# A new order for all operations and loads of a gated linear-attention kernel with a maxout layer

## The chip, the cores and the metric

The kernel runs on one core of a Trainium2 chip. The core has five engines, each with its own queue, which they work through in order and in parallel to one another: TensorE (PE: matmuls and transposes, results in PSUM), VectorE (DVE), ScalarE (ACT), GpSimd (POOL, which works on SBUF only here) and SyncE (SP), which here issues every DMA. They wait for one another through semaphores. The metric is device time in microseconds, as the median of several runs.

## What is computed

A recurrent attention with a state of 48x48 per batch and head, and a feed-forward layer on its output. The sizes are batch 4, 8 heads, 768 steps, head width 48; 3072 tokens of width 384 go into a layer of width 1024.

```python
for t in range(S):
    kt, vt, rt, wt = (k[:, :, t], v[:, :, t], r[:, :, t], w[:, :, t])
    cur = np.einsum('bhd,bhe->bhde', u[None] * kt, vt)
    y[:, :, t] = np.einsum('bhd,bhde->bhe', rt, state + cur)
    state = wt[:, :, :, None] * state + np.einsum('bhd,bhe->bhde', kt, vt)
x = y.transpose(0, 2, 1, 3).reshape(B * S, H * D)
out = np.maximum(x @ w1, x @ w2) @ w_out
```

The kernel does the recurrence in pieces of 256 steps: logarithms of `w` are summed with a triangular matrix, `r` and `k` are scaled by the exponentials of these sums, and what is left are matmuls inside the piece and one product with the state of the pieces before it. For the layer it uses max(a, b) = max(a - b, 0) + b: the weights w1 - w2 (`wd_sb`) go through a relu, and w2 @ w_out is folded into one matrix (`wc_sb`).

## The kernel before

The work is cut into eight units (`UNITS`): units 0 to 3 are the first 256 steps of one batch each, units 4 and 5 the second 256 steps of two batches each, units 6 and 7 the third. Unit 0 is cut into two halves of four heads. What each engine does, and in which order, stands in one list, `ORDER`, written out in the file; the loop at the end of `_body` takes one entry after the other and emits its instructions. An engine's queue is thus the entries of that engine in the order of the list; SP's queue is the order of the loads and stores. An entry is a name, numbers, and for some a letter behind `@` that names the engine: a for ACT, d for DVE, p for POOL.

The entries, with unit u, batch b of the unit, half y:

- `load.u.w` (and k, r, v; `load.0.w.0` and `load.0.w.1` are the halves): L372. `wload.x.n` loads rows n of w1 or w2 (L285), `woload` w_out (L290), `os` stores (L743). All are on SP. `row` and `wl` take a row of sums through DRAM onto partitions.
- `zero`, `mask`, `tri`, `ident`, `identb`, `identq`: constants and cleared areas. `zero.s.1` clears a half of `S_b` (L263), `zero.M` the off-diagonal part of a score buffer.
- `wp` multiplies two steps' w, `ln` takes the logarithm (L387), `hi` and `lo` split it into two parts for units 3 to 7, `ex` is the triangular sum on PE (L398, or L395 and L396 in two parts), `mz` adds (L440), `e0` and `ie` are exponentials, `wt` and `we` give the decay of the whole piece.
- `rw`, `kw` multiply r and k by w; `rk`, `ru`, `dg` make the term with u (products on DVE or POOL, a sum on DVE), which `dd` and `di` place on a diagonal of the score buffer M; `vb` casts v.
- `scale.u.x.b.y` scales r (x = 0) or k (x = 1); for r one input is in PSUM, for k both are in SBUF. `tr` transposes r and k on PE for units 0 to 4 and `te` copies that from PSUM (`RK`); units 5 to 7 use a transposing DMA instead (`dt`, L582).
- `sc` makes scores (L641), `mk` copies them with a mask into M (L650), `kv` updates the state (L596), followed by `st`, `sm`, `sb`; `ya` (L688) and `yi` (L675) make the output, `xe` copies it from PSUM as bf16.
- `wdiff` makes w1 - w2, `w2turn` and `w2take` transpose w2 (L307), `wocast` casts w_out, `wfold` makes the folded matrix (L318) and `wctake` copies it. `gt` is the first product of the layer (L706), `rl` its relu (L717 on ACT, L719 on DVE), `op` the second product (L725 and L729), `oe` its copy from PSUM.
- `hot.8.n` is a group of eight matmuls whose result nobody reads (L234). There are six of them.

PSUM is shared out in two kinds of tiles, four banks "G" for `hot`, `ex`, `tr`, `w2turn`, `wfold`, `gt`, `op`, and two double banks "Y" for `sc`, `kv` and the output. A new tile takes the bank whose last reader stands earliest in `ORDER` and waits for that reader.

A product on POOL of 768 elements or more is split in two (`by_two`), on DVE it is not:

```python
        if e == "d" or n < 2 * HD:
            op(o, a, b)
        else:
            m = o.shape[1] // 2
            for g in (slice(0, m), slice(m, 2 * m)):
                op(o[:, g], a[:, g], b[:, g])
```

Of the kernel before, what the change touches and what calls it, by code (L numbers as in the profile page):

```python
# [797 lines left out]
```

## Time and profile before

| | |
|---|---|
| median of 3 runs | 152.08 us (151.09 to 153.25) |
| the profiled execution | 149.86 us |
| its span, first to last instruction | 148.2 us |
| mean granted clock of TensorE | 0.977 |
| ACT busy | 93.7 us (63%) |
| POOL busy | 76.4 us (52%) |
| read from HBM, written | 23.61 MB, 4.73 MB |
| DMA queue of the loads and stores | 81.6% of 16 engines' span |

The profiled execution is one run of its own, and it was shorter than the three timed ones; all views below are of it. In the views, a busy PE need not be PE at its peak, since matmuls are pipelined. The page gives the busy share of each engine in forty slices of the span, each digit in tenths. The chain that ended last is followed back from the last instruction, at each step to what released it. "issue" in it is time in which the engine waited for nothing that the profile shows.

### The profile page before, as it was taken

The page shows a single profiled execution, that of the slowest core. Times are in us where ns is not written, and L with a number is a line of the kernel's source. Part 1 is how long each engine was busy: PE and PEld are TensorE (multiplying, and loading weights), DVE is VectorE, ACT ScalarE, POOL GpSimd, SP SyncE. Part 2 cuts the span into 40 slices and gives each one's busy share as a digit, 9 for nine tenths or more (in the row PEclk, how much of TensorE's full clock was granted, in tenths as well). Part 3 has the DMA queues.
Part 4 walks back from the last instruction along what each step waited for, and adds up shares of the span by engine and source line. Part 5 has one row for each costly group of instructions (what it writes and reads, how often), then busy time and mean ns, then how long its engine had stood idle before and what let it go on. Part 6 is the DMA issues. An engine that isn't in the chain of part 4 may idle for free.

```text
span 148.2 us, 5523 instructions
## 1 busy us (share of the span) xinstructions
PE 137.9 (93%) x2404; PEld 85.0 (57%) x2404; DVE 115.0 (78%) x160; ACT 93.7 (63%) x173; POOL 76.4 (52%) x94
## 2 busy tenths in 40 slices
PE   4969969989989999999999999999999999999991
PEld 1344654765766676777665456654567445664550
DVE  2259849979999989999999999999599879623100
ACT  3252295679963999998779945578557772245321
POOL 8769729591393047337993069970899600000000
PEclk9996895999999999999999999999999999999999
DMA  4999999989989953999839879999894688360042
GB/s 110 297 357 302 338 269 374 372 247 269 250 234 287 237 123 87 316 286 215 223 68 245 179 170 272 286 233 282 186 250 131 90 172 241 110 214 5 0 164 106
DMA packets 71188, 31.85 MB, mean 215 GB/s; under 512 B 66294, under 2 KB 70391, under 8 KB 71163
## 3 DMA queue, kind: packets, MB, share of 16 engines
q1 hardware_dynamic: 71162, 31.49, 81.6%
q8 instruction: 19, 0.31, 0.9%
q14 instruction: 7, 0.05, 0.1%
HBM read 23.61 MB, written 4.73 MB: 191 GB/s over the span
## 4 chain that ended last, share of the span: by engine, by line
PE 62%; DVE 13%; ACT 7%; DMA 5%; POOL 4%; issue 4%; SPq 2%; POOLq 1%; DVEq 0%; ACTq 0%
PE G L706 15%; PE G L729 15%; PE G L234 7%; PE G L725 6%; DVE M L650 5%; PE Y L688 4%; PE Y L641 3%; DMA lw<-in_w_dram 3%; PE G L318 3%; ACT RK L168 3%; DMA RK<-rp 2%; PE Y L675 2%; PE G L398 2%; POOL kp L180 2%; PE Y L596 1%
## 5 line engine op out<-in xcount | busy, mean ns | idle before, releaser
L729 PE MATMUL G<-wo_sb,gT 128*128 128x384 bf16 x192 | 35.1, 326 | 0.0
L706 PE MATMUL G<-xT,wd_sb 128*128 128x256 bf16 (+1 forms) x192 | 33.9, 326 | 0.1
L650 DVE CAST_PREDICATED M<-mask,Y 128x1024 bf16<-128x1024 int32 (+1 forms) x26 | 28.7, 1133 | 3.0 <-PE Y L641 2.9
L717 ACT ACTIVATE gT<-G 128x512 bf16<-128x512 f32 x41 | 23.4, 599 | 6.2 <-PE G L706 5.9
L729 PEld LDWEIGHTS <-gT 128*128 128x128 bf16 x192 | 18.8, 98 | 12.4
L706 PEld LDWEIGHTS <-wd_sb 128*128 128x128 bf16 x192 | 18.1, 98 | 12.5 <-issue 0.5
L180 POOL TENSOR_TENSOR rku<-rku,u_b 128x384 f32<-128x384 f32 x12 | 12.5, 1065 | 13.1 <-DVE rku L176 13.1
L234 PE MATMUL G<-S_b 128*128 128x512 bf16 x48 | 15.4, 488 | 2.1 <-DVE S_b L263 2.1
L725 PE MATMUL G<-wc_sb,xT 128*128 128x384 bf16 x72 | 15.7, 328 | 0.0
L168 ACT COPY RK<-G 128x1024 bf16<-128x1024 bf16 x12 | 11.8, 1016 | 6.0 <-PE G L565 6.0
L168 ACT COPY osb<-G 128x384 f32<-128x384 f32 x13 | 6.2, 477 | 12.7 <-PE G L729 10.8
L180 POOL TENSOR_TENSOR kp<-lk,iE 128x384 bf16<-128x384 f32 x10 | 11.2, 1147 | 1.8 <-issue 1.8
L234 PEld LDWEIGHTS <-S_b 128*128 128x128 bf16 x48 | 5.6, 123 | 11.0 <-issue 6.6
L168 ACT CAST xT<-Y 128x768 bf16<-128x768 f32 x10 | 10.2, 1033 | 2.4 <-PE Y L688 1.4
L502 DVE TENSOR_REDUCE dg<-rku 128x16 f32<-128x768 f32 x12 | 11.0, 944 | 0.0
L180 POOL TENSOR_TENSOR lk<-lk,lw 128x384 f32<-128x384 f32 x6 | 6.3, 1070 | 7.4 <-DVE rku L176 7.4
L641 PE MATMUL Y<-RK 48*64 48x128 bf16 x384 | 8.9, 220 | 1.2 <-ACT RK L168 0.5
L516 DVE TENSOR_TENSOR M<-identq,gd 128x512 int32<-128x512 int32 x12 | 9.0, 753 | 1.2 <-ACT gd L168 1.0
L440 DVE TENSOR_TENSOR MZ<-G,lg 128x384 f32<-128x384 f32 (+1 forms) x13 | 6.5, 513 | 3.6 <-PE G L398 2.1
L641 PEld LDWEIGHTS <-RK 48*64 48x64 bf16 x384 | 6.3, 106 | 4.9 <-issue 3.2
L688 PE MATMUL Y<-M,vp 64*32 64x128 bf16 x768 | 8.7, 219 | 0.3 <-DVE M L650 0.3
L176 DVE TENSOR_TENSOR rp<-lr,G 128x768 bf16<-128x768 f32 (+2 forms) x11 | 8.7, 795 | 0.4 <-ACT W L486 0.3
(108 smaller groups left out, 234.7 us busy)
## 6 DMA issues: line engine op xcount, KB each, us to landing
lk<-in_k_dram SPq DMA_DIRECT2D x12, 384.0 KB, 4.2
lv<-in_v_dram SPq DMA_DIRECT2D x12, 384.0 KB, 5.9
lr<-in_r_dram SPq DMA_DIRECT2D x10, 384.0 KB, 5.7
lw<-in_w_dram SPq DMA_DIRECT2D x9, 384.0 KB, 5.9
out_dram<-osb SPq DMA_DIRECT2D x14, 192.0 KB, 2.3
gT<-in_moe_w_dram SPq DMA_DIRECT2D x4, 512.0 KB, 8.7
out_dram<-wb SPq DMA_DIRECT2D x10, 192.0 KB, 3.8
wso<-in_moe_w_out_dram SPq DMA_DIRECT2D x4, 384.0 KB, 6.2
```

What stands on the lines that cost most here:

```text
L168: (nc.scalar.copy if e == "a" else nc.vector.tensor_copy if e == "d" else nc.gpsimd.tensor_copy)(o, i)
L180: op(o[:, g], a[:, g], b[:, g])
L234: nc.tensor.matmul(t, zz[:, 0:P], zz[:, 0:512], start=True, stop=True)
L502: nc.vector.reduce_sum(s.dg[:, b].rearrange("p i h -> p h i"), s.rku[:, b], axis=AX.X)
L516: (nc.vector if en == "d" else nc.gpsimd).tensor_tensor(out=o, in0=m, in1=g.unsqueeze(3).to_broadcast([P, 2, H, Q // 2]), op=ALU.bitwise_and)
L641: nc.tensor.matmul(t[q * Q:(q + 1) * Q, e, p * P:(p + 1) * P].rearrange("s (i g) -> s i g", i=2), s.kT[d, b, j, y * n + p, q, :], s.rT[d, ...
L650: nc.vector.copy_predicated(t[:, :, 2 * n * y:2 * n * (y + 1)].rearrange("s i (p e) g -> s p e i g", e=2), mask[:, j].bitcast(I32).unsquee ...
L688: nc.tensor.matmul(lhsT=s.vp[g, b, 2 * p + e, j, m * 32:(m + 1) * 32], rhs=s.M[b, j][g, :, 2 * p + e, :], **into(s, b, q, p * 96 + (e + m) ...
L706: nc.tensor.matmul(t[:, m * n * P:(m + 1) * n * P].rearrange("c (b t) -> c b t", t=P), wd_sb[:, ko, fo * P:(fo + 1) * P], s.xT[:, 0:n, ko, :],
L717: nc.scalar.activation(o, i, AF.Relu)
L725: nc.tensor.matmul(t[:, 0:HD], s.xT[:, a, ko, :], wc_sb[:, ko, :], start=(ko == 0), stop=False)
L729: nc.tensor.matmul(t[:, 0:HD], s.gT[:, c:c + P], wo_sb[:, f, :], start=False, stop=(f == FO - 1))
```

## The change

Only the list `ORDER` is replaced. It has the same 652 entries before and after, in another order. 70 of them go to another engine: 21 from ACT to DVE, 16 from DVE to ACT, 15 from DVE to POOL, 12 from POOL to DVE, 3 from POOL to ACT and 3 from ACT to POOL. The order of the loads on SP changes with it: `load.0.w.1` comes first instead of fifth. Because the bank of a PSUM tile follows from the list, the bank that an operation waits for can be another one. In the part that is not shown, `scale.4.1.1.0`, `scale.5.1.0.0`, `scale.5.1.1.0`, `scale.6.1.0.0`, `rk.7.0` and `rw.7.0` go from DVE to POOL, and `rk.5.0`, `ru.6.0`, `ru.6.1`, `ru.7.1`, `kw.7.0` and `scale.7.1.1.0` from POOL to DVE; the other moves there are copies, casts and relus, mostly between ACT and DVE. The first part of the two lists, to where unit 4 begins, and their ends:

```diff
@@ -51,66 +51,66 @@
 ORDER = """
-zero.k.1@p zero.M.1@p load.1.w.0 zero.m@p mask zero.k.0@d load.0.w.0 u ident identb@p identq@a tri
-wp.0.0@p ln.0.0 zero.s.0@d hot.8.3 zero.o@p load.0.k wp.1.0@d load.0.w.1 load.0.r wp.0.1@d hot.8.0
-kw.0.1@p ln.0.1 ex.0.1 load.1.k ex.0.0 ln.1.0 wload.1.1 kw.0.0@p mz.0.0 ie.0.0 zero.v.1@d wt.0.0
-uspread mz.0.1 ie.0.1 e0.0.1 zero.v.0@d wt.0.1 rw.0.1@d rk.0.0@d scale.0.0.0.1@d utake@a hot.8.2
-we.0.0 load.1.r hot.8.1 rw.0.0@p ru.0.0@d zero.r@d e0.0.0 scale.0.0.0.0@d we.0.1 scale.0.1.0.1@p
-scale.0.1.0.0@p ex.1.0 load.2.w.0 tr.0.0.0 zero.s.1@p te.0.0.0@a tr.0.0.1 te.0.0.1@a w2turn.1.0
-load.0.v vb.0.0@a vb.0.1@p dg.0 load.1.v rk.1.0@d dd.0@a ru.1.0@d mz.1.0 sc.0.0.0.0 wload.1.2 kv.0
-dg.1 ie.1.0 w2take.1.0@a sc.0.0.1.0 kw.1.0@p w2turn.2.0 load.3.w.0 wp.2.0@d vb.1.0@a st.0.0@a ln.2.0
-di.0.0@d zero.M.0@p st.0.1 rw.1.0@d load.2.r wt.1.0 mk.0.0.0.0 sm.0@p w2take.2.0@a sc.0.0.1.1
-sc.0.0.0.1 mk.0.0.0.1 mk.0.0.1.1 ex.2.0 we.1.0 e0.1.0 hot.8.5 vb.1.1@a dd.1@a zero.v.2@d sb.0.0@a
-mz.2.0 scale.1.1.0.0@p scale.1.0.0.0@d ie.2.0 load.2.k rk.2.0@d w2turn.2.1 w2take.2.1@a tr.1.0.1
-kw.2.0@d e0.2.0 wload.1.0 rw.2.0@d kv.1 tr.1.0.0 woload.0 w2turn.1.1 te.1.0.1@a te.1.0.0@a
-w2turn.0.0 mk.0.0.1.0 scale.2.0.0.0@d st.1.0@a st.1.1 sb.1.0@a w2take.1.1@a sc.1.0.0.0 wp.3.0@p
-sc.1.0.1.0 scale.2.1.0.0@p tr.2.0.0 wload.0.2 sb.0.1@a tr.2.0.1 te.2.0.1@a wdiff.2@p load.2.v
-di.1.0@d mk.1.0.1.0 ln.3.0 wload.0.0 w2turn.0.1 w2take.0.1@a mk.1.0.0.0 trih@a vb.2.1@p ya.0.0.1.1
-vb.2.0@a yi.0.0 ya.0.0.0.0 sb.1.1@a ya.0.0.1.0 ya.0.0.0.1 w2take.0.0@d xe.0.0@a ya.1.0.1.0 hi.3@a
-ya.1.0.0.0 hot.8.4 yi.1.0 wdiff.0@d wload.0.1 wdiff.1@d gt.0.2 te.2.0.0@a lo.3@d gt.0.1 ex.3.0
-ru.2.0@d xe.1.0@a rl.0.2@a row.2 sm.1@d gt.1.1 load.3.r load.3.k rk.3.0@d gt.1.3 woload.2 mz.3.0
-wocast.0@a rl.0.1@a ie.3.0 sc.2.0.1.0 woload.1 dg.2 dd.2@a rl.1.3@d kv.2 rl.1.1@d gt.0.3 st.2.0@a
-rl.0.3@a woload.3 gt.1.0 st.2.1 gt.1.2 zero.M.2@p di.2.0@d e0.3.0 rw.3.0@p wocast.2@p load.3.v
-sc.2.0.0.0 scale.3.0.0.0@d kw.3.0@p mk.2.0.0.0 gt.0.0 mk.2.0.1.0 ru.3.0@d wocast.1@p wocast.3@a
-sb.2.0@a wfold.1 load.4.w.0 wp.4.0@d rl.1.0@a wfold.0 rl.1.2@a vb.3.1@d dg.3 wctake.0@a sb.2.1@a
-scale.3.1.0.0@p wfold.2 ln.4.0 hi.4@d wctake.2@a dd.3@d ya.2.0.1.0 wctake.1@a di.3.0@d lo.4@d
-rl.0.0@a row.3 ya.2.0.0.0 load.4.k load.4.r rk.4.0@d vb.3.0@p yi.2.0 kv.3 st.3.0@a st.3.1 xe.2.0@a
-tr.3.0.0 te.3.0.0@a op.1.1 rk.4.1@d oe.1.1@a tr.3.0.1 te.3.0.1@a gt.2.0 gt.2.2 rl.2.2@a rw.4.0@d
-gt.2.1 ru.4.1@p load.4.v wl.2 load.5.w.0 rl.2.1@a ex.4.0 mz.4.0 ex.4.1 wl.3 mz.4.1 row.4 rl.2.0@a
...
-xe.7.0@d gt.7.7 rl.7.7@a gt.7.0 gt.7.4 rl.7.4@a gt.7.5 gt.7.6 rl.7.5@a gt.7.2 rl.7.0@a rl.7.6@d
-os.6.3 os.6.0 gt.7.1 rl.7.1@a os.5.3 os.4.0 gt.7.3 rl.7.3@a rl.7.2@d op.7.1 oe.7.1@d os.7.1 op.7.2
-oe.7.2@a op.7.0 os.7.2 oe.7.0@a os.6.1 os.7.0 op.7.3 oe.7.3@a os.7.3
+zero.m@p load.0.w.1 load.1.w.0 u zero.o@p ident tri identb@p zero.r@d zero.k.1@p zero.s.0@d identq@a
+load.0.r hot.8.3 zero.s.1@p wp.0.1@p load.0.w.0 wp.1.0@d load.0.k load.1.k hot.8.0 zero.k.0@d ln.0.1
+ex.0.1 wp.0.0@d ln.0.0 uspread mz.0.1 e0.0.1 kw.0.0@d rw.0.0@p rk.0.0@d ex.0.0 ln.1.0 rw.0.1@p
+utake@a mz.0.0 kw.0.1@p ru.0.0@p zero.v.1@d wt.0.1 we.0.1 scale.0.0.0.1@d mask ex.1.0 ie.0.0 wt.0.0
+ie.0.1 mz.1.0 we.0.0 scale.0.1.0.1@d e0.0.0 hot.8.1 load.1.r tr.0.0.1 rk.1.0@d scale.0.0.0.0@d
+ru.1.0@p ie.1.0 scale.0.1.0.0@d dg.0 te.0.0.1@a kw.1.0@p dd.0@a wload.1.2 di.0.0@d zero.M.0@p wt.1.0
+we.1.0 hot.8.2 sc.0.0.0.1 load.0.v vb.0.0@a dg.1 e0.1.0 vb.0.1@a kv.0 load.1.v vb.1.1@a w2turn.2.0
+load.2.w.0 wp.2.0@d load.2.r st.0.0@a load.3.w.0 scale.1.1.0.0@p w2turn.2.1 dd.1@a rw.1.0@d
+scale.1.0.0.0@d sc.0.0.1.1 sb.0.1@a load.2.k st.0.1 ln.2.0 wload.1.0 tr.0.0.0 zero.v.0@d mk.0.0.0.1
+wload.1.1 wload.0.1 wp.3.0@p mk.0.0.1.1 wload.0.2 sb.0.0@d w2take.2.1@a vb.1.0@a ex.2.0 tr.1.0.0
+wload.0.0 kv.1 mz.2.0 te.0.0.0@a sc.0.0.1.0 load.2.v sc.0.0.0.0 rk.2.0@d zero.M.1@p rw.2.0@d
+w2take.2.0@a tr.1.0.1 sm.0@p kw.2.0@p st.1.0@a te.1.0.0@a st.1.1 ie.2.0 scale.2.1.0.0@p sb.1.0@a
+mk.0.0.1.0 e0.2.0 hot.8.5 w2turn.1.0 wdiff.2@p w2turn.0.1 mk.0.0.0.0 te.1.0.1@a row.2 w2take.1.0@a
+di.1.0@d w2take.0.1@a sc.1.0.0.0 scale.2.0.0.0@d sc.1.0.1.0 w2turn.0.0 mk.1.0.1.0 sb.1.1@a
+mk.1.0.0.0 w2turn.1.1 wdiff.1@d w2take.1.1@a tr.2.0.1 tr.2.0.0 zero.M.2@p wdiff.0@d te.2.0.0@a
+yi.1.0 ya.1.0.1.0 woload.0 yi.0.0 te.2.0.1@a vb.2.1@d ya.0.0.0.0 sm.1@d ya.0.0.1.1 ya.0.0.0.1
+ya.1.0.0.0 ya.0.0.1.0 load.3.r load.3.k woload.1 woload.2 hot.8.4 ru.2.0@d ln.3.0 hi.3@a lo.3@d
+rk.3.0@d xe.1.0@a kw.3.0@p gt.1.3 gt.1.0 w2take.0.0@a xe.0.0@a trih@a dg.2 gt.0.1 wocast.1@p
+rl.1.3@a rl.0.1@a vb.2.0@a rl.1.0@a ex.3.0 load.3.v mz.3.0 wocast.2@p gt.0.2 rl.0.2@d sc.2.0.1.0
+e0.3.0 woload.3 rw.3.0@d kv.2 wocast.0@a st.2.0@a ru.3.0@p gt.1.1 rl.1.1@a st.2.1 wocast.3@a gt.1.2
+ie.3.0 scale.3.1.0.0@p gt.0.3 load.4.w.0 wp.4.0@p dd.2@d sc.2.0.0.0 scale.3.0.0.0@d di.2.0@d
+mk.2.0.0.0 gt.0.0 wfold.2 vb.3.0@a rl.1.2@a dg.3 wfold.0 rl.0.3@a sb.2.1@a wctake.2@a rl.0.0@a
+wfold.1 row.3 dd.3@d tr.3.0.1 mk.2.0.1.0 wctake.1@d load.4.k load.4.r wl.2 tr.3.0.0 sb.2.0@a
+di.3.0@d ln.4.0 wctake.0@a hi.4@d ya.2.0.0.0 ya.2.0.1.0 load.4.v vb.3.1@p wl.3 load.5.w.0 yi.2.0
+rk.4.0@d kv.3 te.3.0.0@a xe.2.0@a st.3.0@a te.3.0.1@a lo.4@d op.1.1 ex.4.0 gt.2.0 oe.1.1@a rk.4.1@d
...
+oe.6.0@a yi.7.0 xe.7.0@a yi.7.1 xe.7.1@d op.6.1 oe.6.1@a os.6.1 oe.6.3@d gt.7.0 gt.7.3 rl.7.3@d
+os.6.0 rl.7.0@a os.6.3 gt.7.2 rl.7.2@a gt.7.7 rl.7.7@d gt.7.1 rl.7.1@d gt.7.6 rl.7.6@d gt.7.4 gt.7.5
+os.4.2 rl.7.5@d rl.7.4@a op.7.1 op.7.3 oe.7.3@d os.7.3 op.7.0 oe.7.0@a oe.7.1@a os.7.0 os.7.1 op.7.2
+oe.7.2@a os.7.2
 """.split()
```

62 lines of the change are left out of this document (31 added, 31 removed).

## The prediction

> **What bounds the kernel now.** I read the profile page first, then busy time by stretches of the span, then the chain that ended last, and last the timeline of the first 48 us. The page (lines of its first two parts):
>
> ```profile
> PE 137.9 (93%) x2404; PEld 85.0 (57%) x2404; DVE 115.0 (78%) x160; ACT 93.7 (63%) x173; POOL 76.4 (52%) x94
> PE   4969969989989999999999999999999999999991
> DVE  2259849979999989999999999999599879623100
> ```
>
> TensorE is busy for 93% of 148.2 us; its gaps lie in the first quarter. Busy time by stretches (PE, PEld, DVE, ACT, POOL, then granted clock, DMA share, GB/s) says how sharp that is:
>
> ```profile
> 12.00:16.00 4.00, 4.00 (x13) 1.41 (x12) 3.96 (x8) 0.17 (x1) 4.00 (x6) 0.57 1.13 309
> 24.00:28.00 4.00, 4.00 (x54) 2.17 (x52) 3.97 (x10) 1.24 (x3) 2.24 (x3) 0.75 1.07 373
> 36.86:144.93 108.07, 106.45 (x1978) 66.93 (x1978) 89.30 (x113) 72.78 (x127) 51.01 (x51) 1.00 0.79 192
> ```
>
> From 36.86, the first product with the folded first weight (L706), to 144.93, the last matmul, PE idles 1.62 us in 108.07. Before that the clock falls twice. The chain that ended last (start, us, what):
>
> ```profile
> 11.42 5.16 PE G L234 x16
> ...
> 36.86 0.78 PE G L706 x6
> ...
> 40.58 0.65 issue
> ...
> 118.08 3.68 DMA RK<-rp
> ...
> 144.96 0.48 ACT wb L168
> ```
>
> L234 is the filler ("hot"): 5.16 us of it sits on the chain while `ex.1.0` (L398) is queued behind. So the time is the start of the packed stretch (36.86), the stretch, and a tail of 3.2 us (144.96 to 148.2). The profiled execution took 149.86 us, 1.66 more than its span and 2.22 under the median of 152.08; I take the difference from the profile and put it on the median.
>
> **The change, part by part.** Both lists hold the same 652 operations, so no work goes. After the first L706 product the same products follow, but for `yi.1.0` (12 small matmuls), which moves ahead of it. Two things can change the time: when that product starts, and what stalls in the packed stretch. The tail ends in `op`, a copy on ACT and one store in both: nothing.
>
> *First loads.* The rows of the timeline (start, us, engine, line, what, idle before and its releaser):
>
> ```profile
> 2.06 5.30 PE L234 MATMUL G<-S_b 128*128 128x512 bf16 x16 [2.06 <-DVE S_b L263]
> 4.21 0.56 DVE L176 TENSOR_TENSOR lg<-lw 128x384 f32<-128x384 f32 x1 [2.20 <-DMA lw<-in_w_dram]
> 5.86 0.59 POOL L176 TENSOR_TENSOR lg<-lw 128x192 f32<-128x192 f32 x1
> 7.12 0.36 DVE L176 TENSOR_TENSOR lg<-lw 128x192 f32<-128x192 f32 x1 [2.36 <-DMA lw<-in_w_dram]
> 7.52 0.78 ACT L387 ACTIVATE lg<-lg 128x192 f32<-128x192 f32 x2 [0.67 <-DVE lg L176]
> 8.03 0.89 PE L398 MATMUL G<-lg,tri 128*128 128x192 f32 x4 [0.66 <-ACT lg L387]
> 14.00 1.38 POOL L263 MEMSET S_b<- 128x1536 bf16 x1
> ```
>
> `load.0.w.1` goes from fifth to first in SP's queue: it lands by about 4.2 (the first load now does) instead of 7.12. But its `wp.0.1` goes to POOL, behind set-up fills that now include the 1.38 us clearing of S_b, and `load.0.w.0` becomes fifth, with the same bytes ahead of it as `load.0.w.1` had: 7.1 again. POOL reached `wp.0.0` at 5.86; without zero.M.1 and the mask, with zero.s.1, it reaches `wp.0.1` near 4.7. With 0.59 and a logarithm of 0.39, and even a wait on DVE's own product, `ex.0.1` is ready by 6.4. The sixteen fillers hold PE to 7.2. So 8.03 becomes 7.2: 0.8 us of the 2.9 the load gives.
>
> *The middle of the front.* `ex.1.0` now stands ahead of the fillers hot.8.1 and hot.8.2, so it leaves at about 9.4 instead of 16.42. What is late next is POOL: it is given `ru.0.0` and `ru.1.0`, which DVE did, and loses the products `scale.0.1.0.*`. Rows:
>
> ```profile
> 10.29 0.94 DVE L176 TENSOR_TENSOR rku<-lr,lk 128x768 f32<-128x768 f32 x1
> 10.42 1.27 POOL L176 TENSOR_TENSOR kp<-lw,iE 128x192 bf16<-128x192 f32 x1 [1.17 <-ACT iE L460]
> 11.53 0.35 DVE L176 TENSOR_TENSOR rp<-lr,G 128x192 bf16<-128x192 f32 x1 [0.29 <-ACT W L486]
> 11.65 0.59 POOL L176 TENSOR_TENSOR kp<-lk,iE 128x192 bf16<-128x192 f32 x1
> 2.79 1.39 POOL L186 TENSOR_SCALAR_AFFINE_SELECT mask<-mask 64x64 f32<-64x64 f32 x6
> 20.95 0.95 POOL L257 MEMSET M<- 128x1024 bf16 x1 [3.39 <-DVE M L516]
> 23.83 1.00 POOL L176 TENSOR_TENSOR kp<-lk,iE 128x384 bf16<-128x384 f32 x1
> L180 POOL TENSOR_TENSOR rku<-rku,u_b 128x384 f32<-128x384 f32 x12 | 12.5, 1065 | 13.1 <-DVE rku L176 13.1
> ```
>
> POOL's list from about 10.3 (when `kw.0.1` is through) is ru.0.0 2.13, mask 1.7 (1.39 and its fill of 0.31), ru.1.0 2.13, kw.1.0 1.0, zero.M.0 0.95, scale.1.1.0.0 2.0: 9.9 us, to 20.2. That is the good end. The first two POOL rows give the bad one: a 128x192 product takes 0.59 beside a DVE product that reads PSUM (11.53), and 1.27 beside one with both inputs in SBUF (10.29): it loses about 0.7 of that one's 0.94. Four such DVE operations now fall on this list (scale.0.1.0.1, scale.0.1.0.0, both about 0.65, rk.1.0 0.94, di.0.0 0.7), so it ends up to 2.7 later, at 22.9. I take 22.9, because the rows for just this pairing show the loss. The Trainium skill's page "SBUF — State Buffer" says that a DVE instruction with two SBUF inputs shuts out a GpSimd instruction that reads SBUF for its whole length, and one with at most one does not. These rows agree (1.27 against 0.59); by the full block the list would end at about 23.1 and the sum be -2.2.
>
> `scale.1.1.0.0` gates `tr.1.0.0`, and behind that ACT works without a pause:
>
> ```profile
> L168 ACT COPY RK<-G 128x1024 bf16<-128x1024 bf16 x12 | 11.8, 1016 | 6.0 <-PE G L565 6.0
> L168 ACT CAST wb<-G 128x512 bf16<-128x512 f32 x5 | 2.9, 582 | 1.7 <-PE G L307 1.7
> L168 ACT CAST xT<-Y 128x768 bf16<-128x768 f32 x10 | 10.2, 1033 | 2.4 <-PE Y L688 1.4 <-PE Y L675 1.0
> 34.46 2.35 DVE L176 TENSOR_TENSOR wd_sb<-gT 128x1024 bf16<-128x1024 f32 x2
> 29.67 2.96 POOL L180 TENSOR_TENSOR wd_sb<-wst 128x512 bf16<-128x512 f32 x2
> ```
>
> Four `te` of 1.0, three `w2take` of 0.58, seven copies and exponentials of 0.34 to 0.53 (3.1 together), `xe.1.0` 1.03: 9.9 us, after 1.0 us for `tr.1.0.0` and `kv.1`, and I add 0.5 for the filler hot.8.5 in front of `w2turn.1.0`. So the first L706 product starts at 22.9 + 11.4 = 34.3 (at 20.2 it would be 31.6, but the same 0.5 grows to 1.9 if the filler falls in a half-clock stretch: 33.0). DVE has its `wdiff` by then: the three products ru.0.0, ru.1.0 and w2take.0.0 that it loses (2.8 us together) outweigh the halves it gains, and I get 33.9 for wdiff.0; wdiff.2 on POOL, blocked meanwhile, 34.3. Weights landed well before in the old run (the two `wdiff` on DVE waited for nothing), and fewer bytes stand ahead of the last one now. **Front: 36.8 to 34.3, minus 2.5; ends 0 and minus 3.8.**
>
> *The packed stretch.* The 0.65 inside `kv.2` (chain at 40.58) is "issue": no engine and no transfer released it, so I leave it where it is, at nothing. The 0.3 or so that PE waits after the transfer of `RK` (chain at 118.08) should go: its chain ran through POOL's two scalings of unit 7, and the second goes to DVE. A new wait stands at `ex.4.0`: three L706 products that came before it come after it, and its `wp.4.0` moves to POOL:
>
> ```profile
> 47.51 0.94 DVE L176 TENSOR_TENSOR lg<-lw 128x768 f32<-128x768 f32 x1
> 62.49 1.95 POOL L180 TENSOR_TENSOR lg<-wso 128x384 f32<-128x384 f32 x2
> 43.00 2.41 POOL L180 TENSOR_TENSOR kp<-lk,iE 128x384 bf16<-128x384 f32 x2
> 50.79 0.95 DVE L413 SCALAR_TENSOR_TENSOR wst<-lg,wst 128x768 f16<-128x768 f32 x1
> ```
>
> 0.94 becomes 1.95, behind a scaling of 2.41 that itself waits for `ie.3.0`. I get wp.4.0 at 46.3 and what follows it (a logarithm of some 0.8, hi 0.6, then rk.4.0 and lo of 0.95 on DVE, and a pause of 0.5) at 50.1. PE is there at 49.3: 34.3, then the 8.1 us that the old run took from its first L706 product to `wfold` less one small product, three `wfold`, two `tr`, unit 2's `ya` and `yi`, `kv.3`, `op.1.1`, 15 in all. Cost 0.8; nothing if POOL is on time. Everything on PE is queued behind it, so the stall is paid in full. DVE gives up wp.4.0, ru.3.0, scale.4.1.1.0 and both scale.5.1 (0.95 each, as at 47.51) and takes rk.5.0, rw.3.0 and some relus and copies (about 4): lighter by a little under 1 us, of which I count 0.4 as gained, since DVE stands on the chain only from 55 to 75. The other swaps of copies between ACT and DVE (0.5 to 0.7 either way) lie beside packed PE work: nothing, while each stays ahead of its bank's next use.
>
> **Sum:** -2.5 (front) - 0.3 (RK) + 0.8 (ex.4.0) - 0.4 (DVE) = -2.4 us; 149.86 becomes 147.5, and 152.08 becomes 149.7.
>
> **Rivals.** *POOL is on time* (its reads miss the four DVE operations): the front gives 3.8 and `ex.4.0` costs nothing: -3.8 - 0.3 - 0.4 = -4.5, 147.6. For it: blocking was seen on POOL products alone, and the mask is six short selects. *The front gives nearly nothing*: POOL slips 2 us more than I count, since the mask beside rk.1.0 is not shown in the old run: -0.4, 151.7. A third half-clock stretch in the front costs about as much: eight fillers take 3.4 us at 0.43 each (of the 16 in 5.30, half were slow) instead of 1.7: -0.7, 151.4. The Trainium skill's page "TensorE: Matmul & The Clock Gate", Part 1, has the clock halve after a window of some 3.4 us without work, counted freely of the kernel; the stretches at 0.57 and 0.75 agree in kind, and by it a third is possible as the front keeps its pauses. *Slower*: `wp.4.0`. It ended at 48.45 on DVE; if POOL ends it 5.5 us later than my 46.3, at 51.8, PE stands that much longer at `ex.4.0` and the sum passes +3: 155.2 and up, about 156. For it: POOL is the slower engine there by a factor of two and has five operations ahead of it. Against it: from 34.3 these are some 10 us with one late input, `ie.3.0`. *The change does nothing*, because the mask, the clock and POOL together give back the 2.4: 152.
>
> **How the numbers follow.** Main case 0.46 (148.2 to 151.0), POOL on time 0.20, the front gives nearly nothing (POOL, clock, or no effect) 0.26, slower 0.08. The likeliest gives 149.7. About 2% is what a measurement of this kernel can tell from no change: below 149.04 lie the case on time and some 0.4 of the main one, 0.38; above 155.1 lies 0.07; between them 0.55. The range, 146.8 to 153.0, runs from below the case on time to past no change, by about the 1 us by which runs of one kernel differ from their median (151.09 to 153.25); what it leaves out is the slower case and the tails.
>
> **What would show it.** Right: the first L398 near 7.2; `ex.1.0` ahead of the fillers; POOL's rku products at 128x384 taking over 1.0 each before 18; first L706 near 34; a wait of PE on L395 after the first `op`; no wait of PE on `RK` in unit 7. Wrong: first L706 after 36, or idle PE over 3 us behind it.

## The result, and the profile after

The changed kernel took 151.53 us (median of 20 runs, 149.92 to 156.79); the kernel before, on the same chip, 150.37 us (20 runs, 148.4 to 153.25). The ratio is 1.0151, 95% interval 1.0117 to 1.0185. It is taken over undisturbed executions alone, here and below, and so need not be the quotient of the medians. The forecast was 149.7, a gain of 2.4 us; the change costs 1.5% by the ratio, some 2 us, and 1.2 us by the two medians. The profiled execution of after took 151.67 us, its span 150.0 us (before: 149.86 and 148.2).

The first lines of the page of after, and its rows of PE and of the granted clock:

```profile
PE 137.7 (92%) x2401; PEld 84.6 (56%) x2404; DVE 119.4 (80%) x164; ACT 92.8 (62%) x168; POOL 84.1 (56%) x99
PE   4979998869999999999939999999999999999991
PEclk9995999999999999999996899999999999999999
```

In before the gaps of TensorE lay in the first quarter. Here there is a 3 in the middle (slice 21, from 75 us), and behind it the clock falls to 6 and 8 tenths. Read beside each other, the starts of the same operations in both timelines (an ordinary table, us; operations counted off against `ORDER`) say when the lead came and went:

```
operation            before    after    lead of after
ex.0.1 (L398)          8.03     6.96     1.07
ex.1.0 (L398)         16.42     9.25     7.17
first L706            36.79    35.27     1.52
op.3.0 (L725)         74.98    72.09     2.89
op.3.1 (L725)         78.34    79.02    -0.68
kv.5                  85.74    87.13    -1.39
last matmul, its end 144.93   146.77    -1.84
```

At 72 us after led by 2.89. Between `op.3.0` and `kv.5` it lost 4.28. The two orders are not quite level at these two places: when `op.3.0` starts, before has already done the 64 matmuls of `ya.4.1` (0.75 us) that after does later, and when `kv.5` starts, before has done `gt.4.5` and `ex.6.0` (1.07 us). Like for like the lead went from 2.1 to -2.5, and some 0.6 of this came back behind `kv.5`. The timeline of PE in after over that place (start, us, line, what, idle before and its releaser):

```profile
72.58 1.46 PE L729 MATMUL G<-wo_sb,gT 128*128 128x384 bf16 x8
73.98 0.53 PE L675 MATMUL Y<-RK,S_b 128*32 128x128 bf16 x24
74.44 0.42 PE L688 MATMUL Y<-M,vp 64*32 64x128 bf16 x32
75.08 0.43 PE L688 MATMUL Y<-M,vp 64*32 64x128 bf16 x32 [0.22 <-DVE M L650]
75.44 0.53 PE L675 MATMUL Y<-RK,S_b 128*32 128x128 bf16 x24
75.90 0.57 PE L688 MATMUL Y<-M,vp 64*32 64x128 bf16 x43
78.74 0.35 PE L688 MATMUL Y<-M,vp 64*32 64x128 bf16 x21 [2.28 <-issue]
79.02 0.66 PE L725 MATMUL G<-wc_sb,xT 128*128 128x384 bf16 x3
79.52 2.21 PE L729 MATMUL G<-wo_sb,gT 128*128 128x384 bf16 x8
```

And the same work in before:

```profile
73.72 0.75 PE L688 MATMUL Y<-M,vp 64*32 64x128 bf16 x64
...
74.98 0.66 PE L725 MATMUL G<-wc_sb,xT 128*128 128x384 bf16 x3
75.48 1.46 PE L729 MATMUL G<-wo_sb,gT 128*128 128x384 bf16 x8
76.87 0.86 PE L675 MATMUL Y<-RK,S_b 128*32 128x128 bf16 x48
77.67 0.75 PE L688 MATMUL Y<-M,vp 64*32 64x128 bf16 x64
78.34 0.66 PE L725 MATMUL G<-wc_sb,xT 128*128 128x384 bf16 x3
78.84 1.46 PE L729 MATMUL G<-wo_sb,gT 128*128 128x384 bf16 x8
```

The old list had 64 of the small matmuls of `ya.4` (L688), then `op.3.0`, then the rest. The new one has all 176 small ones of `ya.4` and `yi.4` in a row. In the middle of one operation, after 43 of 64 like matmuls with the same inputs, TensorE stands idle for 2.28 us (a "stand", from here on), and the releaser is "issue": no engine, no transfer. Then `op.3.1` takes 2.50 instead of 1.80 and the products behind it are slow too. The window of after from 80 to 84 us (PE, PEld, DVE, ACT, POOL, then granted clock, DMA share, GB/s) shows why:

```profile
80.00:84.00 4.00, 4.00 (x14) 1.66 (x12) 2.20 (x5) 2.03 (x4) 0.00 (x0) 0.57 0.86 144
```

and the same window of before:

```profile
80.00:84.00 4.00, 4.00 (x20) 1.84 (x19) 4.00 (x7) 3.61 (x9) 0.00 (x0) 1.00 1.26 186
```

14 matmuls instead of 20, at a clock of 0.57.

**Where the stands lie.** The page shows that TensorE's instructions themselves come by DMA (queue, kind: packets, MB, share):

```profile
q8 instruction: 19, 0.31, 0.9%
```

0.31 MB in 19 packets is 16 KB each; 2404 matmuls and as many weight loads are 4808 instructions, 253 a packet. I counted the instructions of TensorE ahead of every stand named issue of 0.3 us or more in the timelines of PE of this study: 35 of them, in 15 of the 17 traces. The count modulo 256 (what is left over after division by 256) lies between 178 and 186 in all 35 (the same place, but for a few missing records). So the stands lie at the bounds between blocks of 256 instructions. And each ends 1.23 to 1.59 us after a packet of this queue has ended. Nine of the 35 (us, from the trace's DMA records; "own work" is the time from the entry into the block of 256 to the stand):

```
kernel, place       entered   packet starts   ends    TensorE goes on   stand   own work
before, kv.2         34.03       38.49       39.79        41.23         0.65     6.55
after, ya.0          27.07       30.36       31.49        32.78         0.80     4.91
after, ya.4          74.45       76.47       77.44        78.74         2.28     2.01
a_again, ya.4        74.34       76.55       77.50        78.90         2.87     1.69
a_op31, ya.4         72.70       75.22       76.16        77.67         1.12     3.85
a_load7late, ya.4    74.56       75.06       76.51        77.98         1.74     1.69
b_dense, ya.4        73.49       75.05       76.47        77.91         2.53     1.89
a_halves, yi.6      110.11      111.09      112.09       113.46         1.71     1.64
b_shift72, yi.6     128.09      128.99      129.96       131.25         1.71     1.45
```

So the theory (A): the next block is asked for only when TensorE has entered the one before it; ahead of these 35 stands the packet started 0 to 4.5 us after that, took 0.9 to 1.45, and 1.2 to 1.6 later the block ran. A block with less work than this sum leaves TensorE standing, above all one of 128 small matmuls. The rivals: (B) a late operand that the profile doesn't name, (C) the clock gate (what lowers the granted clock) stopping TensorE by itself.

The first clause of A is too strong. In `after` three of the 19 packets started 0.3 to 3.1 us before TensorE entered the block (the last one at 141.90, the entry at 144.97). And four short blocks of 1.6 to 1.8 us of work did not stand, or for no more than 0.24 us: those at unit 5 in `a_again`, `a_kfirst`, `after` and `a_load7late`, where the packet had started 0.3 to 0.8 us before the entry. So the work in a block alone does not decide; when its packet starts does too, and what starts it is not shown.

### The profile page after: what moved, and what is told of

Its sections match the earlier page's. It is cut to its first block, busy times and chain, and to the rows that moved or that the text cites. A ratio compares the mean times of both kernels' runs of the same rounds, so it can differ in the third digit from the quotient of the medians.

```text
span 150.0 us, 5532 instructions
## 1 busy us (share of the span) xinstructions
PE 137.7 (92%) x2401; PEld 84.6 (56%) x2404; DVE 119.4 (80%) x164; ACT 92.8 (62%) x168; POOL 84.1 (56%) x99
## 4 chain that ended last, share of the span: by engine, by line
PE 59%; DVE 12%; DMA 10%; issue 7%; POOL 5%; SPq 3%; ACT 2%; DVEq 0%; POOLq 0%
PE G L706 19%; PE G L729 15%; PE G L725 6%; DVE M L650 6%; PE Y L688 4%; DMA lv<-in_v_dram 4%; DMA lk<-in_k_dram 4%; PE Y L641 3%; PE G L234 3%; SPq L372 3%; DMA WL<-row 2%; POOL lg L180 2%; PE Y L675 2%; PE Y L596 1%; DVE rku L176 1%
## 5 line engine op out<-in xcount | busy, mean ns | idle before, releaser
L706 PE MATMUL G<-xT,wd_sb 128*128 128x256 bf16 (+1 forms) x192 | 34.8, 332 | 0.0
L717 ACT ACTIVATE gT<-G 128x512 bf16<-128x512 f32 x39 | 22.5, 598 | 14.4 <-PE G L706 14.0
L706 PEld LDWEIGHTS <-wd_sb 128*128 128x128 bf16 x192 | 18.7, 99 | 13.5 <-issue 2.0
L180 POOL TENSOR_TENSOR kp<-lk,iE 128x384 bf16<-128x384 f32 x16 | 17.2, 1101 | 3.1 <-DVE lk L176 1.5
L234 PE MATMUL G<-S_b 128*128 128x512 bf16 x45 | 13.9, 454 | 2.2 <-DVE S_b L263 2.1
L688 PE MATMUL Y<-M,vp 64*32 64x128 bf16 x768 | 9.4, 219 | 3.6 <-issue 3.3
L516 DVE TENSOR_TENSOR M<-identq,gd 128x512 int32<-128x512 int32 x12 | 10.8, 918 | 0.5 <-ACT gd L168 0.5
L168 ACT COPY osb<-G 128x384 f32<-128x384 f32 x11 | 5.2, 476 | 9.5 <-PE G L729 9.4
L688 PEld LDWEIGHTS <-vp 64*32 64x32 bf16 x768 | 7.0, 90 | 6.2 <-issue 5.4
L176 POOL TENSOR_TENSOR S_f<-T,W 128x192 f32<-128x192 f32 (+1 forms) x5 | 3.4, 689 | 11.4 <-ACT W L488 8.1
L387 ACT ACTIVATE lg<-lg 128x768 f32<-128x768 f32 (+2 forms) x9 | 5.6, 625 | 6.5 <-DVE lg L176 2.7
L719 DVE TENSOR_SCALAR gT<-G 128x512 bf16<-128x512 f32 x9 | 6.1, 689 | 3.2 <-PE G L706 3.1
```

The lines of the kernel that those rows point to most:

```text
L168: (nc.scalar.copy if e == "a" else nc.vector.tensor_copy if e == "d" else nc.gpsimd.tensor_copy)(o, i)
L234: nc.tensor.matmul(t, zz[:, 0:P], zz[:, 0:512], start=True, stop=True)
L516: (nc.vector if en == "d" else nc.gpsimd).tensor_tensor(out=o, in0=m, in1=g.unsqueeze(3).to_broadcast([P, 2, H, Q // 2]), op=ALU.bitwise_and)
L688: nc.tensor.matmul(lhsT=s.vp[g, b, 2 * p + e, j, m * 32:(m + 1) * 32], rhs=s.M[b, j][g, :, 2 * p + e, :], **into(s, b, q, p * 96 + (e + m) ...
L706: nc.tensor.matmul(t[:, m * n * P:(m + 1) * n * P].rearrange("c (b t) -> c b t", t=P), wd_sb[:, ko, fo * P:(fo + 1) * P], s.xT[:, 0:n, ko, :],
L717: nc.scalar.activation(o, i, AF.Relu)
```

## Experiments

**1. Another place in the order, another count.** First, one larger operation moved into the row:

```diff
-ya.4.1.0.0 yi.4.1
...
-ya.4.1.1.0 op.3.1
+ya.4.1.0.0 op.3.1 yi.4.1
...
+ya.4.1.1.0
```

> The kernel after, with one entry of the list moved: op.3.1 (11 matmuls, 1.8 us) stands between ya.4.1.0.0 and yi.4.1 instead of behind ya.4.1.1.0. Theory A, supply of instructions: TensorE's instructions come in blocks of 256 (128 matmuls with their weight loads; 19 packets of 16 KB on the DMA's instruction queue), the fetch of the next block starts only when TensorE has entered the one before it, and takes about 3 to 4 us until that block can start; in the kernel after, one block consists of the small matmuls of ya.4 and yi.4 alone and is used up in 2.0 us, so TensorE stands for 2.28 us. With op.3.1 in this block it takes 3.9 us: the stand falls below 0.7 us, the half clock behind it goes, and the time is 147.5 to 149, a ratio to before of 0.98 to 0.99. Theory B, a late operand (a copy or a scaling that the profile does not name): the stand stays near 2.3 us in front of the last ya, 151.5 us. Theory C, the clock gate itself stops TensorE after a long stretch at full clock: it stays between 76 and 80 us of the span, 151.5 us.

Second, the order left alone and only the count shifted, in `hot`, for the groups `hot.8.3` and `hot.8.0` (this is the edit in after; in before it has 37 in the place of 25):

```diff
-        for _ in range(n):
+        few = {3: 25, 0: 25}.get(_, 0)
+        for _ in range(n - (1 if few else 0)):
             nc.tensor.matmul(t, zz[:, 0:P], zz[:, 0:512], start=True, stop=True)
+        for _ in range(few):
+            nc.tensor.matmul(t[0:32, 0:128], zz[0:64, 0:32], zz[0:64, 0:128], start=True, stop=True)
```

> The kernel after, order unchanged; in the first two filler groups one matmul of eight becomes 25 small ones of 64x32 by 128 columns, so that 48 more matmuls (96 instructions) stand ahead of everything that follows, at about the same time. Theory A: the bounds of the blocks of 256 lie 48 matmuls earlier; the block that ends among the ya.4 now has op.3.0 in it and takes 3.5 us: no stand over 0.7 us between 74 and 80 us. By the same count the block that ends near 112 (unit 6) has 1.4 us of work and gets a stand of 1 to 2.5 us that it did not have; in all 149 to 151 us, ratio 0.99 to 1.005. Theories B and C: the stand of 2.3 us stays where it is, and none comes near 112: 151.5 us.

> The kernel before, order unchanged, with 72 more small matmuls (144 instructions) in the first two filler groups, in the place of one filler matmul each. Theory A: before has by luck no block with under 3.5 us of work; 72 matmuls further three blocks have 1.6, 1.2 and 1.3 us of work, and end near 34.5, 112 and 129 us. Each gets a stand of 1.5 to 2.5 us named issue, partly with half clock behind it: 154 to 158 us, ratio 1.025 to 1.05. Theories B and C: no stand at these places, since nothing of the order or of the operands has changed: 150.4 us, ratio 1.00.

`a_op31`: the stand fell from 2.28 to 1.12 (below 0.7 was expected), and the clock stayed at 1.0. The profiled execution took 148.71, but the median was 150.66, ratio 1.0026 (0.9913 to 1.0139): the time that was expected, 147.5 to 149, was missed. Part of the reason stands in its timeline of PE: at 79.28, behind the last `ya`, TensorE now waits 1.18 us for ACT's copy `xT`, which `op.3.1` had covered at its old place. In `a_shift48` no stand was left among the `ya.4`, and one of 2.23 came among the `yi.6`, where the count had put it. In `b_shift72`, with not one operation of the layer or the recurrence moved, stands of 3.73, 1.71 and 1.91 came in the three blocks named ahead of the run (at later times, since its front was slower). The row of the stand in the timeline of PE of `a_shift48`:

```profile
115.63 0.52 PE L678 MATMUL Y<-RK,S_b 128*32 128x128 bf16 x22 [2.23 <-issue]
```

and the three in that of `b_shift72`:

```profile
50.26 0.23 PE L691 MATMUL Y<-M,vp 64*32 64x128 bf16 x1 [3.73 <-issue]
...
131.25 0.86 PE L678 MATMUL Y<-RK,S_b 128*32 128x128 bf16 x46 [1.71 <-issue]
...
150.60 0.23 PE L691 MATMUL Y<-M,vp 64*32 64x128 bf16 x2 [1.91 <-issue]
```

(L678 and L691 are L675 and L688 behind the three added lines.) B and C give no reason why stands should move with a count. The times of these two (152.43 and 162.39 us) price nothing: my 37 small fillers took 4.1 us, more than those they replaced, and in `a_shift48` the clock halved in the front. So the shift was made again without cost, each filler of 512 columns as two of 256:

```diff
-        for _ in range(n):
-            nc.tensor.matmul(t, zz[:, 0:P], zz[:, 0:512], start=True, stop=True)
+        for i in range(2 * n):
+            nc.tensor.matmul(t[:, i % 2 * 256:][:, 0:256], zz[:, 0:P], zz[:, 0:256], start=True, stop=True)
```

> The kernel after, unchanged, as the measure for the others on this chip: a stand of about 2.3 us named issue among the ya.4 near 76 us and one of 0.8 near 32, ratio to before 1.01 to 1.02. Theory A (supply of instructions in blocks of 256) has them at the same place in every execution; if the 2.3 us was an accident of one execution, it is missing here.

> The kernel after; each filler matmul of 512 columns is two of 256, so the fillers take the same time with 48 more matmuls in all (96 instructions). Order, operands and all other work are unchanged. Theory A: as the bounds of the blocks move by 48 matmuls, the stands near 32 (0.8) and 76 (2.3) go, with the half clock behind the latter, and one of 1.5 to 2.5 us comes near 111, where a block now has 1.4 us of work: 0.5 to 2.5 us below after on the same chip. Theories B (late operand) and C (clock gate): the stands stay at 32 and 76 and none comes at 111; the time is that of after.

> The kernel before with the same halved fillers (48 more matmuls at no filler time). Theory A: a block with 1.4 us of work ends near 112 us, and a stand of 1.5 to 2.5 us comes there that before does not have; the 0.65 at 40.6 goes: 1 to 2.5 us above before, ratio 1.005 to 1.017. Theories B and C: no change, ratio 1.00. It also takes out what the small fillers of the run with 72 more matmuls cost in the front.

After, run again unchanged: 151.87 us, ratio 1.0215 (1.0099 to 1.0332), the stand 2.87 at the same matmul. With halved fillers: 149.83 us, ratio 1.0026 (0.9966 to 1.0086), 2.0 us less by the medians with the same order. The rows of PE of `a_halves`, at unit 4 and at unit 6:

```profile
75.30 0.76 PE L688 MATMUL Y<-M,vp 64*32 64x128 bf16 x64
75.99 0.66 PE L725 MATMUL G<-wc_sb,xT 128*128 128x384 bf16 x3
...
111.18 0.57 PE L675 MATMUL Y<-RK,S_b 128*32 128x128 bf16 x26
113.46 0.52 PE L675 MATMUL Y<-RK,S_b 128*32 128x128 bf16 x22 [1.71 <-issue]
```

The 64 small matmuls that were cut by 2.28 us run through, and the stand is where the new bound is. It was not all as expected: of the 0.80 in the front a stand of 1.25 remained, now in the first L706 products. In before the same edit brought stands of 2.05, 0.98 and 3.10, the first and the last with half clock behind them. Its four runs lie between 151.11 and 158.18 us (median 155.34, against 150.37), too far apart for a ratio; that it is slower by more than the 1 to 2.5 us expected is not shown.

**2. The row alone, put into before.**

```diff
-oe.2.0@a ya.4.1.0.0 ya.4.1.1.0 os.2.0
+oe.2.0@a os.2.0
...
-op.3.0 e0.5.0
+op.3.0 ya.4.1.0.0 ya.4.1.1.0 e0.5.0
```

> The kernel before with two entries moved: ya.4.1.0.0 and ya.4.1.1.0 (64 small matmuls) from ahead of sc.4.0.0.0 to behind op.3.0, so that all of ya.4 and yi.4 stand together as in the kernel after. Theory A (supply): the block of 256 instructions that begins among them then holds small matmuls alone, 1.8 us of work, and TensorE gets a stand named issue of 1.5 to 3 us there that before does not have, in some executions with half clock behind it: 1.5 to 4 us above before, ratio 1.01 to 1.027. If the loss of after came from another part of its order, this move costs nothing: ratio 1.00.

152.07 us against 150.97, ratio 1.0126 (1.004 to 1.0211). The timeline of its PE:

```profile
73.34 0.75 PE L688 MATMUL Y<-M,vp 64*32 64x128 bf16 x64
74.01 0.86 PE L675 MATMUL Y<-RK,S_b 128*32 128x128 bf16 x48
74.81 0.57 PE L688 MATMUL Y<-M,vp 64*32 64x128 bf16 x43
77.91 0.35 PE L688 MATMUL Y<-M,vp 64*32 64x128 bf16 x21 [2.53 <-issue]
78.19 1.03 PE L725 MATMUL G<-wc_sb,xT 128*128 128x384 bf16 x3
79.02 2.77 PE L729 MATMUL G<-wo_sb,gT 128*128 128x384 bf16 x8
```

Two entries of 652, moved past 2.2 us of other work, make the old kernel lose at this place what the new one loses, with the slow products behind it. This is the cause of the loss at unit 4.

**3. What makes the packet late.** In after, `load.7.w.0` fills the DMA engines from 74.5 us, when the block is entered.

```diff
-scale.5.0.1.0@d load.7.w.0 yi.4.0
+scale.5.0.1.0@d yi.4.0
...
-os.2.0 rk.6.1@d
+os.2.0 load.7.w.0 rk.6.1@d
```

> The kernel after with one load moved on SP's queue: load.7.w.0 (768 KB, needed some 20 us later) behind os.2.0 instead of ahead of wl.4. In the trace of after it is issued at 73.1 and fills the DMA engines from 74.5; TensorE enters the block of ya.4 at 74.45, and the packet with the next block starts only 2.02 us later. Theory A with contention: the packet queues behind that load; without it, it starts within 0.6 us, and the stand of 2.28 falls to 0.5 to 1.0 us, the half clock behind it goes, 148 to 149.5 us, 2 us or more below after on the same chip. If the packet's delay has nothing to do with the load (a fixed time of the supply), the stand stays at 2.0 to 2.3 us and the time at that of after.

The packet started 0.51 us after the entry, as expected; in the five traces of after and its variants with the load beside this block, it took 2.02 to 2.52. But the stand only fell to 1.74, since the packet itself took 1.45, and 1.47 more passed until TensorE went on: 0.51 + 1.45 + 1.47 = 3.43 against 1.69 of work. Half clock followed, and 151.77 us is no gain on 151.87. The load beside it explains part of the delay; a block of 1.7 us stands without it too. Both remedies together:

> The kernel after with both remedies at unit 4: op.3.1 behind ya.4.1.0.0, and load.7.w.0 behind os.2.0 on SP. Alone the first left a stand of 1.1 us, the packet starting 2.5 us after its block was entered, beside the load; alone the second left 1.7, the packet starting after 0.5. Together, if the two add up, the block takes 3.9 us and the next can start 3.4 after its entry: no stand over 0.3 us at unit 4, 147.5 to 149.5 us, ratio 0.985 to 1.00, and 2 to 3 below after. If after loses elsewhere in its rest, it stays above 150.5.

No stand at unit 4, ratio 0.9977 (0.9919 to 1.0035), 150.68 us: what after had lost against before is regained, but not the lead. The remedies have costs of their own, and the largest is the one of `a_op31`: behind the last `ya`, at 80.93, the first product (L706) waits 1.7 us, until ACT has copied `xT` (the row names a product on DVE that ends at the same time); `op.3.1` had covered this. There are also 0.8 us for `RK<-kp`, whose transfer now stands beside the load, and stands of 0.97 and 1.06 at other blocks. Rows of the waits of this run's PE (the profiled execution took 152.07 us, more than the median):

```profile
PE Y L688 <- issue: 2.0, 2, 1.1
PE G L706 <- DVE rku L176: 1.7, 1, 1.7
PE Y L641 <- DMA RK<-kp: 0.8, 1, 0.8
```

**4. The front alone.** All entries of after up to `hot.8.4`, then the rest of before in its order; behind the front the blocks fall as in before.

> All entries of the kernel after up to hot.8.4, which stands ahead of its first product of the layer, and behind them what is left in the order of the kernel before. It prices the new front alone, since the blocks of 256 behind it fall as in before. If the front is worth what the traces of the two kernels show at the first L706 product (35.4 against 36.8), 149.0 us, ratio 0.988 to 0.995, and no stand over 1 us behind it. If the lead is lost again to the loads or to a late ex.4.0: 150.4 us, ratio 1.00. If the loss of the kernel after lies in its front after all: above 150.8 us.

> The same kernel as in the run b_afterfront (new front, old rest), for a narrower interval. By the traces the front is worth 1.8 us at the first L706 product (34.9 against 36.8) and nothing behind it takes this back: 148 to 149 us, ratio 0.985 to 0.997. If the lead is lost again on the way: ratio 1.00.

148.13 us against 151.35, ratio 0.9965 (0.9886 to 1.0045), unclear; then, run again, 147.59 against 150.97, ratio 0.9795 (0.9718 to 0.9872). The two intervals do not overlap, so the size of the gain is open between nothing and 2.8%; by the second run the new front is a gain, and in neither run is it a loss. Its first L706 product stands at 34.96 and 35.06, its longest stand was 0.87 and 0.61, and its slices of PE (second run) have no 3:

```profile
PE   4999789769999999999999999899999999999991
PEclk9999999999999999999999999999999999999998
```

What sets the front? In the five traces with the new front that there were then, the first L706 product came 26.0 to 26.4 us behind `kw.0.0` on DVE, which began between 8.41 and 9.50. Loads reordered so that k lands sooner:

```diff
-load.0.w.1 load.1.w.0 u
...
-load.0.r hot.8.3 zero.s.1@p wp.0.1@p load.0.w.0 wp.1.0@d load.0.k load.1.k
+load.0.w.1 u load.0.w.0 load.0.k load.0.r load.1.w.0
...
+rk.0.0@d wp.1.0@d
```

> The kernel after with the same order of the first loads and wp.1.0 behind rk.0.0 on DVE, nothing else changed: kw.0.0 starts before 8.0 us on DVE, the first mk of unit 1 18.9 to 20.2 us behind it and the first L706 product at 33.5 to 34.4 (34.4 to 35.6 in the runs so far), if DVE from the landing of k sets the front. If POOL's list sets it, as the prediction had it, L706 stays at 34.4 or later.

`kw.0.0` began at 8.14 instead of 8.97, but the first L706 came at 35.86: `wp.1.0` behind `rk.0.0` made `ex.1.0` late (PE waited 1.8 us for its logarithm), and the sum behind it on DVE came at 12.67 instead of 11.73. No gain, in this one execution; the landing of k is not the only input of that time. The stand at unit 4 was 3.09.

**5. Larger matmuls among the small ones everywhere.**

```diff
-ya.0.0.0.0 sm.1@d
+ya.0.0.0.0 hot.8.4 sm.1@d
...
+ya.5.1.1.0 op.4.1
...
-yi.5.0 op.4.1
+yi.5.0
```

These in the kernel of `b_afterfront`, the same with the loads of `a_kfirst`, and in after both `hot.8.4` and `op.3.1` moved as shown and `op.4.1` behind `yi.5.0`:

> The kernel with the new front and the old rest, with two entries moved so that larger matmuls stand among the small ones: hot.8.4 behind ya.0.0.0.0 and op.4.1 behind ya.5.1.1.0. Theory A: the two stands it had, 0.75 near 32 us and 0.87 near 93, go; the first L706 product comes 0.5 to 0.8 us sooner; 146 to 147.5 us, ratio to before 0.97 to 0.985. If the stands were hidden by late operands anyway: 147.8, the time of the same kernel without the moves.

> The kernel of the run b_frontspread with the first loads in the order load.0.w.1, u, load.0.w.0, load.0.k, load.0.r, load.1.w.0, and wp.1.0 behind rk.0.0 on DVE. In five runs with the new front, the first product of lk and lw on DVE (kw.0.0) starts between 8.41 and 9.50 us, when load.0.k has landed, and the first mk of unit 1 follows exactly 20.0 us later: DVE, not POOL, sets the front. Then k 1.2 us sooner brings the first L706 product 0.5 to 1.1 us forward against b_frontspread: 145.3 to 146.8 us. If POOL or ACT sets it, no gain.

> The kernel after with three entries moved: op.3.1 behind ya.4.1.0.0, hot.8.4 behind ya.0.0.0.0, op.4.1 behind yi.5.0. Theory A: the stands named issue in the ya (together 3.3 us or more in after, and half clock behind the longest) shrink to under 1.2 us in all; what is left of after is then what the prediction summed up without them: 146.5 to 148.5 us, ratio 0.975 to 0.99. If after had other losses in its rest, it stays above 150.

All three missed: 149.31, 150.32 and 151.77 us, ratios 1.0031 (0.9946 to 1.0116), 1.0048 (1.0011 to 1.0084) and 1.0178 (1.0106 to 1.025). Most of the stands went (0.19 is left at `yi.5` in the first, 0.94 at unit 4 in the last), but the moved work had covered something. The rows of PE at `yi.5` of `b_frontspread`:

```profile
95.92 0.55 PE L675 MATMUL Y<-RK,S_b 128*32 128x128 bf16 x25 [0.19 <-issue]
99.00 1.24 PE L706 MATMUL G<-xT,wd_sb 128*128 128x512 bf16 x5 [2.52 <-ACT xT L168]
```

and of `b_afterfront2`:

```profile
93.45 0.41 PE L675 MATMUL Y<-RK,S_b 128*32 128x128 bf16 x14 [0.58 <-issue]
93.79 0.66 PE L725 MATMUL G<-wc_sb,xT 128*128 128x384 bf16 x3
...
95.58 4.05 PE L706 MATMUL G<-xT,wd_sb 128*128 128x512 bf16 x18
```

Behind the last `yi` ACT copies `xT`, and `op.4.1` was what PE did meanwhile. Put earlier, it saves 0.6 and leaves a wait of 2.52. The same happened with `hot.8.4`: in `b_frontspread` the first L706 product waits 1.10 us for `xT` and starts at 36.19 instead of 34.96, and in `a_spread` such waits for `xT` add up to 3.4 us. The earlier loads of `b_frontspread_k` changed nothing (first L706 at 36.35).

## Why the prediction was wrong, point by point

**The step that failed** is in the packed stretch: "The 0.65 inside `kv.2` (chain at 40.58) is 'issue': no engine and no transfer released it, so I leave it where it is, at nothing." The row was read rightly and then dropped. It is the same thing as the 2.28, at a bound of a block (the table above), and it neither stays nor is worth nothing: after has no stand at `kv.2`, and has 0.80 at `ya.0` and 2.28 at `ya.4`. I costed the new order of PE by the duration of each operation, as if its instructions were always there; what an order does to the blocks was a missing term. It is 2.28 for the stand and 1.68 for the half clock behind it (0.70, 0.63 and 0.35 at `op.3.1`, `gt.4.4`, `gt.4.3`), 4.0 in all. The forecast of -2.4 with +4.0 is +1.6, and the two profiles differ by 1.8.

That this comes so close is partly luck. The front gave 1.5 in these profiles and not 2.5, and 0.65 came from the stand at `kv.2` that went, the very term that the sum had at nothing. Together they are the lead of 2.1 at `op.3.0`. It is luck too that the measured 151.53 lies inside the range of 146.8 to 153.0 and beside the 151.7 of a rival: the sum started from 152.08, a median of three runs, where 20 runs gave 150.37, and the change went the other way.

**First loads:** right. 6.96 against the forecast 7.2, the fillers holding PE to the end.

**`ex.1.0` ahead of the fillers:** right, 9.25 against 9.4. What came late next was not POOL alone. The timeline of POOL in after:

```profile
10.86 1.96 POOL L180 TENSOR_TENSOR rku<-rku,u_b 128x384 f32<-128x384 f32 x2 [0.96 <-DVE rku L176]
13.14 2.36 POOL L186 TENSOR_SCALAR_AFFINE_SELECT mask<-mask 64x64 f32<-64x64 f32 x6
15.59 1.95 POOL L180 TENSOR_TENSOR rku<-rku,u_b 128x384 f32<-128x384 f32 x2
17.50 1.45 POOL L176 TENSOR_TENSOR lw<-lk,lw 128x384 f32<-128x384 f32 x1
20.74 1.01 POOL L176 TENSOR_TENSOR kp<-lk,iE 128x384 bf16<-128x384 f32 x1
```

The list ended at 21.75, between my ends of 20.2 and 22.9: the mask took 2.36 instead of 1.39 and `kw.1.0` 1.45 instead of the 1.00 of the sum, while the `rku` products were not slowed (0.98 each, where I had named over 1.0). Beside those two pairs DVE was the one that lost, which the sum did not have: one product of `scale.0.1.0.1` took 0.82 at 12.21, against 0.38 for the same shape at 14.66, and `di.0.0` took 1.37 at 16.71, against 0.69 in before. My 22.9 was also too late by its own rows: 0.7 lost of 0.94 is 2.2 on four operations of 2.9 together, not 2.7. The rule that I quoted from the Trainium skill, page "SBUF — State Buffer", would have given 23.1.

**From `tr.1.0.0` to the first L706, "plus 11.4":** undersized. It took 13.9 (21.40 to 35.27): not ACT but DVE held it, and the chain that ended last names it (start, us, what):

```profile
3.59 5.28 DMA lk<-in_k_dram
...
25.82 1.28 DVE M L650 x2
...
28.91 2.35 DVE M L650 x2
31.98 0.80 issue
32.78 0.82 PE Y L688 x65
33.98 1.46 PE G L234 x6
35.44 1.97 PE G L706 x18
```

and 0.80 of it is a stand for instructions among the `ya`. The front gave 1.52 in this execution, where 2.5 was summed. In `a_op31`, `a_again` and `a_load7late`, which have the same front, it gave 1.2 to 2.4 (first L706 at 34.41 to 35.58), and in `a_op31_load7`, with half clock from 33.21, nothing (36.85). One trace prices little here: `b_dense` has the old front, and its first L706 stands at 35.27 as well, since it has one stretch of half clock ahead of it where before has two. With the old rest, the new front gained 0.35% (not clear of zero) and 2.05% in two runs.

**RK, unit 7:** right in kind, PE has no wait for `RK` in after. **`ex.4.0`:** the new wait is there and small, 0.30 where 0.8 was taken (L396 starts 0.46 behind L395, 0.16 in before). **DVE lighter by 0.4:** wrong in sign, the page has 119.4 us busy against 115.0; it cost PE next to nothing behind the front, where the list of its waits has one of 0.2 us besides those named issue.

**The rivals:** none named the cause. The one on half clock was near in kind, but placed it in the front; it came behind the stand. The slower rival through `wp.4.0` did not happen. Of the two signs given for "wrong", the first L706 past 36 did not come (35.27). Idle PE over 3 us behind it did, just: PE was busy for 108.38 of the 111.50 us from 35.27 to the last matmul, so it idled 3.12. Most of that is named issue; the row of PE's waits in after has 3.3 us, 0.80 of them ahead of the first L706:

```profile
PE Y L688 <- issue: 3.3, 3, 2.3
```

So 2.5 us of stands behind the front, and 1.7 of half clock, did the harm.

**What stays open.** With both remedies at unit 4 after equals before, though the new front alone gained in one of its two runs. Named in that profile are the wait of 1.7 that `op.3.1` had covered, 0.8 for `RK<-kp`, a stand of 1.06 at unit 5, and in the front a stand of 0.97 with half clock behind it. Whether these make up the whole difference was not tested. Why a packet starts anywhere from 3.1 us before the entry to 4.5 behind it is shown in part, for one load only.

## What to carry to other kernels

A stand of PE named "issue" in the middle of like matmuls is a price, not noise: count the instructions ahead of it, and if such stands fall on one residue modulo 256, treat the supply of instructions as a resource: here a block of 256 that stood had 2.2 to 7.2 us (median 4.7) from its entry to the next one, and of 17 blocks with about 2 us of work or less 11 stood for 1.7 to 3.7 us, two for 0.36 and 1.06, and four for 0.24 or less. When an order is changed, look for rows of small matmuls that come together, or for any edit that shifts the count, since either could cost 2 to 4 us at one place here, stand and half clock together, with the operations themselves unchanged. Before a large operation is moved into such a row, see what it covers where it stands.

## What the runs showed of the hardware that was not expected

The stands above: 35 in 15 of 17 traces, 0.31 to 3.73 us, each ending 1.23 to 1.59 us after a 16 KB packet of instructions. The Trainium skill, page "Runtime: NRT & Kernel Launch", section "Instruction fetch mechanics", says that the stream is refilled in blocks of 256 instructions, the next one fetched while the present one runs, and that crossing a bound is mostly hidden. The runs agree with the size of the block and with the fetch of one block ahead; they do not agree that it is hidden where a block is short: of 17 blocks of about 2 us of work or less, 11 stood for over 1.7 us.

The packet started later beside the kernel's own transfers: 2.02 to 2.52 us after the entry beside the 768 KB of `load.7.w.0` (five traces), 0.49 and 0.51 without it (two traces).

Half clock followed the stands of 1.74, 2.05, 2.28, 2.53, 3.09, 3.10 and 3.73, and one of 0.97 (`a_op31_load7`), and not those of 1.71 (two), 1.91, 2.23 and 2.87. Each of these slow stretches lasted 3.41 us. The Trainium skill, page "TensorE: Matmul & The Clock Gate", Part 1, has windows of some 3.4 us that run freely of the kernel, and the clock falling after an idle one. The runs agree with the length, and with stands of like length that do or do not bring half clock. They do not show that a window has to be idle throughout: in `after` the slow stretch began at 80.09, and the 3.41 us ahead of it hold 2.06 us of the stand and 1.35 us in which TensorE worked.
